# Attention ahead of a mixture of experts on one core: part of the softmax subtraction and of the key sums goes to ScalarE, two buffers for token lists, a new order of issue

## The chip, the cores and the metric

The kernel runs on one core of one Trainium2 chip. The metric is device time in microseconds (us), the median of several runs. The engines are TensorE (PE, with its weight loads shown apart as PEld), VectorE (DVE), ScalarE (ACT), GpSimd (POOL) and SyncE (SP), whose queue issues most transfers. Each engine works through its own instructions in the order in which they were issued, and waits on semaphores for the others.

## What is computed

```python
# q, k, v: 8 x 8 heads x 576 x 64; keys and values are averaged over groups of 8 rows
k_p = k.reshape(B, H, Sp, pool, D).mean(axis=3)
v_p = v.reshape(B, H, Sp, pool, D).mean(axis=3)
scores = scale * np.matmul(q, k_p.transpose(0, 1, 3, 2))
scores = scores - np.max(scores, axis=-1, keepdims=True)
attn = np.exp(scores)
attn = attn / (np.sum(attn, axis=-1, keepdims=True) + 1e-09)
x = np.matmul(attn, v_p)                       # then heads side by side: 8 x 576 x 512
...
logits = x @ w_gate; local_gate = sigmoid(x @ w_local)
# along each sequence: token s takes argmax(logits[s]), or the expert before it if local_gate >= 0.5
h = np.maximum(x[b, s] @ w1[e], 0.0)           # 512 -> 1024
out[b, s] = p[e] * (h @ w2[e])                 # 1024 -> 512, p = softmax(logits)
```

## The kernel before

The work has two halves. **Attention** runs in 20 units (four pairs of batches, five units each: `t` from 0 to 3 is one batch with 128 query rows twice, `t == 4` stacks the remaining rows of both batches). A unit is a chain: `sc` puts its scores into one PSUM tile `sp` of three banks, of which there is one; `mx` takes the row maxima on DVE (864 columns of banks 0 and 1, 288 of bank 2); `sb` subtracts them on DVE from PSUM into `ap`; `ex` takes the exponential on ACT from `ap` into `at`; `T0`, `T1`, `T2` transpose `at` on PE and `T0c`... copy the results to SBUF; `v0`, `v1`, `v2` multiply by the values on PE and `v0c`... copy those; `fs`, `fp`, `fd` scale and store the rows. The same value product gives the routing logits. Beside the units run the keys (`lk` loads, `kp` sums over groups of 8 on DVE into `kd`, and into the half empty tile `kdz`), the values (`lv` loads, `vp` sums on POOL or, as `vp.d`, on DVE, `vt`, `vc`, `vl`, `vd` turn them through the gate weights, `vm` on POOL or `vm.d` on DVE places them into `vaug`), the routing of each pair (`rA`, `rT0` to `rP`), 36 scatters of token numbers (`s`, POOL) and the first expert's weights (`w1`, `w2` load; `p1`, `p2` split each number into a high part, copied on ACT, and a low part, subtracted on POOL, or on DVE as `p1.d`, `p2.d`).

**Experts** follow: blocks of 256 tokens of one expert, `L1` and `L2` for the first, then `M1`, `M2`, then a chain of blocks in `blocks(b)`. Each block's token numbers come by `ids_load` from SP into `idp`, `meta` adds them up on DVE, `gather` fetches the rows, `quarters` and `x_turn` turn them.

What sets the order is a list written out by hand, `PLAN` for attention, `PLAN_B` and `PLAN_C` for the passage to the experts: `do(name, n)` issues step `name` of unit, chunk or pair `n`, in the list's order. A suffix (`.d`, `.p`, `.s`) sets `pick["e"]`, the engine that takes the step. So each engine's queue is the list's steps of that engine, in that order. For instance, around the third pair's routing the list says

```python
v1:14 T1c:15 T2:15 w1:3 vl:21 v1c:14 sc:17 vd:21 T2c:15 ex:16 fs:14 vl:23 ga:0 fp:14 vd:23 p1:2 v0:15 rA:2 T0:16
v0c:15 p1:3 v1:15 T0c:16 T1:16 v1c:15 mx:17 XR:0 v2:15 rT0:2 fd:14 v2c:15 sb:17 T1c:16 rT1:2 vp:22 rS0:2 fs:15
```

Of the kernel before, what the change touches and what calls it, by code (L numbers as in the profile page):

```python
# [16 lines left out]
P = 128  # L17
# [38 lines left out]
wa:0 lv:0 lv:1 lv:2 lk:0 wa:1 lk:1 lk:2 lq:0 lc:0 lq:1 lq:2 lq:3 vp:0 vp.d:2 lv:3 vt:0 vc:0 vm:0 vt:2 kp:0  # L56
vc:2 vm:2 vp:1 lk:3 kp:1 lv:4 vt:1 lv:5 kp:2 vm:1 lk:4 sc:0 lk:5 vl:0 mx:0 lq:4 vc:1 vd:0 sb:0 vl:2 vd:2 ex:0 vl:1
sc:2 vd:1 T0:0 mx:2 T0c:0 T1:0 vp:3 sb:2 v0:0 T1c:0 T2:0 kp:3 v1:0 v0c:0 T2c:0 lv:6 vt:3 v1c:0 v2:0 vm.d:3 vp:5
vc:3 lk:6 vl:3 v2c:0 sc:1 vp:4 ex:2 vd:3 fs:0 vt:5 lq:5 lq:6 T0:2 mx:1 vc:5 fp:0 lv:7 lv:8 vt:4 vl:5 vm.d:5 vc:4
vm:4 T0c:2 vd:5 kp:4 vl:4 fd.p:0 T1:2 vd:4 vp:6 v0:2 kp:5 lk:7 T1c:2 T2:2 v0c:2 v1:2 T2c:2 kp:6 lv:9 lk:8 v1c:2  # L60
v2:2 sb:1 lk:9 vt:6 v2c:2 vm:6 fs:2 ex:1 sc:3 fp:2 vc:6 mx:3 lq:7 T0:1 vp:8 T1:1 T0c:1 sb:3 fd.p:2 v0:1 T1c:1 vp:7
T2:1 kp:7 v1:1 v0c:1 T2c:1 ex:3 v2:1 vp:9 lv:10 lv:11 lk:10 v1c:1 sc:4 v2c:1 T0:3 lq:8 fs:1 vl:6 lv:12 T0c:3 T1:3
vd:6 vt:8 fp:1 mx:4 T1c:3 vm.d:8 vc:8 sb:4 T2:3 fd.p:1 vt:7 T2c:3 kp:8 vl:8 vc:7 sc:5 vm:7 ex:4 vd:8 kp:9 lk:11
v0:3 lq:10 T0:4 v0c:3 mx:5 vp:11 lk:12 v1:3 T0c:4 vp:10 T1:4 sb:5 v1c:3 v2:3 T1c:4 vl:7 v2c:3 vt:9 vd:7 ex:5 vt:11
fs:3 sc:6 lv:14 lv:13 vm:11 vc:11 vm.d:9 vc:9 fp:3 vl:11 lq:9 pf:0 mx:6 T0:5 vt:10 fd.p:3 T0c:5 vd:11 v0:4 kp:10 vc:10
# [38 lines left out]
def moe_attention(ctx: ExitStack, tc: tile.TileContext, q, q_st, k, v, w_gates, w1, w2, out):  # L104
# [23 lines left out]
    scratch_i = const.tile([P, 64], I32, name="scratch_i")  # L128
# [3 lines left out]
    nc.gpsimd.iota(scratch_i[:, 0:2 * E], pattern=[[0, 2], [1, E]], base=0, channel_multiplier=0)  # L132
    nc.vector.tensor_copy(out=iota8, in_=scratch_i[:, 0:2 * E].rearrange("p (b e) -> p b e", b=2))
# [107 lines left out]
    idp = route.tile([P, 4, TB, 2], F32, name="idp", bufs=1)  # L241
# [956 lines left out]
```

## Time and profile before

| what | value |
|---|---|
| median of 3 runs | 669.05 us (664.52 to 671.4) |
| profiled execution, its own time | 667.99 us |
| its span, first to last instruction | 665.9 us |
| PE busy | 614.6 us, 92% of the span |
| DVE busy | 444.5 us, 67% |
| ACT busy | 272.5 us, 41% |
| POOL busy | 249.8 us, 38% |
[...]

The page's picture in 40 slices of 16.6 us shows where the halves differ: PE's digits run between 4 and 9 in the first 13 slices and stand at 9 from there to the end; the granted clock shows 6, 7 and 8 in places of the first 13 slices and full speed after. The chain that ended last is, in the end, the last scatter of output rows (L1063). Idle time of an engine counts only where the bottleneck waits for it, so the views that matter are PE's waits, by stretch.

### The profile page before, as it was taken

To read this page: it belongs to the slowest core of one execution; us is meant where nothing else is said; L and a number is where in the kernel's file an instruction comes from. 1 tells how busy PE (TensorE), PEld (TensorE's weight loads), DVE (VectorE), ACT (ScalarE), POOL (GpSimd) and SP (SyncE) were. 2 spreads that over 40 slices of the span, in tenths; PEclk is the share of its full clock that TensorE was granted. 3 is DMA by queue.
4 is the path that set the end of the run, shared out by engine and by line. 5 is a ranking of instruction groups with operands and counts; after the bars stand their busy time and mean duration, and the time that the engine had idled before them with its cause. 6 is when DMAs were issued, how large, how long until landed. Compare 5 with 4: busy or idle time off the path is not lost. (4 is left out here: it accounts for less than half of the span.)

```text
span 665.9 us, 11834 instructions
## 1 busy us (share of the span) xinstructions
PE 614.6 (92%) x3588; PEld 520.8 (78%) x3588; DVE 444.5 (67%) x1002; ACT 272.5 (41%) x612; POOL 249.8 (38%) x297
## 2 busy tenths in 40 slices
PE   4889898987787999999999999999999999999994
PEld 3777797876575888878888878788887887888883
DVE  7688989887677744454549448578944478954550
ACT  1354454444463242132336226366713266522330
POOL 6477767767475532121112221211222112222102
PEclk9998999976698999999999999999999999999998
DMA  8799946364413036953237644948864329764222
GB/s 326 270 354 343 319 171 206 127 207 128 143 40 104 11 83 173 329 162 114 69 108 240 224 125 109 331 117 320 280 211 126 110 65 335 251 230 121 78 93 61
DMA packets 74966, 120.12 MB, mean 180 GB/s; under 512 B 21486, under 2 KB 42994, under 8 KB 74868
## 3 DMA queue, kind: packets, MB, share of 16 engines
q1 hardware_dynamic: 66196, 96.41, 43.3%
q0 software_dynamic: 8672, 22.59, 10.8%
q8 instruction: 39, 0.64, 0.4%
q14 instruction: 59, 0.48, 0.2%
HBM read 87.85 MB, written 33.22 MB: 182 GB/s over the span
## 5 line engine op out<-in xcount | busy, mean ns | idle before, releaser
L327 PE MATMUL hp<-x,w1h 128*128 128x512 f32 x376 | 135.8, 402 | 0.1
L348 PE MATMUL o_ps<-w2h,ht_h 128*128 128x512 f32 x312 | 122.7, 393 | 1.5 <-PEq L1128 0.9
L348 PE MATMUL o_ps<-w2h,ht_l 128*128 128x512 f32 x312 | 122.0, 391 | 0.0
L348 PE MATMUL o_ps<-w2l,ht_h 128*128 128x512 f32 x312 | 121.6, 390 | 0.0
L306 POOL DMA_INDIRECT kk<-x_rows,mi x44 | 43.9, 997 | 186.7 <-DVE mi L302 172.1
L329 PE MATMUL hp<-x,w1l 128*128 128x256 f32 x376 | 106.2, 282 | 0.4 <-DVE w1l L212 0.4
L334 ACT COPY hs<-hp 128x256 f32<-128x256 f32 x94 | 34.8, 371 | 145.0 <-PE hp L329 143.1
L327 PEld LDWEIGHTS hp<-x,w1h 128*128 128x128 f32 x376 | 71.3, 190 | 17.8 <-DVE hs L335 0.6
L564 PE MATMUL op<-vaug,aT 128*128 128x148 f32 (+4 forms) x448 | 73.9, 326 | 2.1 <-ACT aT L373 1.8
L329 PEld LDWEIGHTS hp<-x,w1l 128*128 128x128 f32 x376 | 71.7, 191 | 1.4 <-DVE w1l L212 0.8
L564 PEld LDWEIGHTS op<-vaug,aT 128*128 128x128 f32 (+1 forms) x448 | 66.0, 193 | 7.9 <-ACT aT L373 3.1
L339 ACT ACTIVATE ht_h<-hs 128x256 fp32r<-128x256 f32 x136 | 57.2, 420 | 34.7 <-DVE hs L335 34.6
L348 PEld LDWEIGHTS o_ps<-w2h,ht_h 128*128 128x128 f32 x312 | 58.6, 188 | 14.6 <-ACT ht_h L960 2.5
L348 PEld LDWEIGHTS o_ps<-w2h,ht_l 128*128 128x128 f32 x312 | 58.6, 188 | 13.4 <-DVE ht_l L961 0.7
L348 PEld LDWEIGHTS o_ps<-w2l,ht_h 128*128 128x128 f32 x312 | 58.6, 188 | 11.5
L340 DVE SCALAR_TENSOR_TENSOR ht_l<-hs,ht_h 128x256 fp32r<-128x256 f32 x136 | 59.2, 435 | 6.3 <-ACT ht_h L339 6.0
L335 DVE TENSOR_TENSOR hs<-hp,hs 128x256 f32<-128x256 f32 x94 | 38.9, 418 | 28.4 <-ACT hs L334 27.6
L1063 POOL DMA_INDIRECT out<-ob,mi x22 | 24.9, 1130 | 72.7 <-DVE ob L1060 33.0
L1060 DVE TENSOR_SCALAR ob<-o_ps,ms 128x512 f32<-128x512 f32 x22 | 16.5, 749 | 52.5 <-PE o_ps L348 51.7
L1063 POOL DMA_INDIRECT out<-vt_in,mi x20 | 23.8, 1192 | 65.7 <-DVE vt_in L1060 19.4
L373 ACT COPY osb<-op 128x444 f32<-128x444 f32 (+2 forms) x56 | 26.5, 476 | 48.1 <-PE op L564 43.6
L700 POOL DMA_INDIRECT ids<-pm,pos x36 | 35.9, 998 | 23.9 <-DVE pos L697 12.7
(245 smaller groups left out, 1129.1 us busy)
## 6 DMA issues: line engine op xcount, KB each, us to landing
raw<-in_moe_w SPq DMA_DIRECT2D x56, 512.0 KB
xd<-kk SPq DMA_DIRECT2D x21, 512.0 KB
kt<-xd SPq DMA_DIRECT2D x84, 128.0 KB
kk<-in_k SPq DMA_DIRECT2D x16, 576.0 KB
vt_in<-in_v SPq DMA_DIRECT2D x16, 512.0 KB
qt<-in_q SPq DMA_DIRECT2D x16, 512.0 KB
x_rows<-xs SPq DMA_DIRECT2D x16, 512.0 KB
vt_in<-in_v SPq DMA_DIRECT2D x16, 128.0 KB
```

The costliest lines, as they stand in the source:

```text
L306: nc.gpsimd.indirect_dma_start(out=xg[b % 2][:, h, :], out_offset=None, in_=x_rows[0:NT + 1], in_offset=bass.IndirectOffsetOnAxis(ap=mi[b ...
L327: nc.tensor.matmul(out=ps, lhsT=W1[0][:, kk, f * P:(f + 1) * P], rhs=xt[:, kk].rearrange("p i n -> p (i n)"), start=(kk == 0), stop=False, ...
L329: nc.tensor.matmul(out=ps[:, 0:2 * P], lhsT=W1[1][:, kk, f * P:(f + 1) * P], rhs=xt[:, kk, 0, :], start=False, stop=(kk == KD - 1), skip_g ...
L334: nc.scalar.copy(out=hb[:, 0, :], in_=ps[:, 2 * P:])
L335: nc.vector.tensor_tensor(out=hb[:, 1, :], in0=ps[:, 0:2 * P], in1=hb[:, 0, :], op=ALU.add)
L339: nc.scalar.activation(out=ht[0][:, f, :], in_=hb, func=AF.Relu)
L340: nc.vector.scalar_tensor_tensor(out=ht[1][:, f, :], in0=hb, scalar=0.0, in1=ht[0][:, f, :].bitcast(F32), op0=ALU.max, op1=ALU.subtract)
L348: nc.tensor.matmul(out=to[h], lhsT=ht[i][:, kk, h * P:(h + 1) * P], rhs=W2[j][:, kk, :], start=(n == 0), stop=(n == 3 * KF - 1))
L373: nc.scalar.copy(out=out, in_=in_)
L564: nc.tensor.matmul(out=out, lhsT=lhs, rhs=rhs if len(out.shape) == 3 else rhs.rearrange("p s x -> p (s x)"), start=all(x[0] != n for x in ...
L700: nc.gpsimd.indirect_dma_start(out=ids[u % 4].rearrange("t m w -> (t m) w"), out_offset=bass.IndirectOffsetOnAxis(ap=pos[:, u:u + 1], axis=0),
L1063: nc.gpsimd.indirect_dma_start(out=outv, out_offset=bass.IndirectOffsetOnAxis(ap=mi[b % NM][:, h:h + 1], axis=0), in_=ob[b % 2][:, h, :], ...
```

## The change

Four things are done. First, a unit's `sb` step may be marked `sb.a`: then DVE subtracts only bank 2 (288 columns), ACT makes a tile `nm` of twelve negated, scaled maxima, and ACT's exponential reads banks 0 and 1 straight from PSUM in twelve instructions of 72 columns, each with its own column of `nm` as bias; ten of the 16 wide units are marked (0, 2, 3, 6, 7, 10, 11, 12, 13, 16). Second, DVE sums all of a key chunk in one instruction of 144 groups, and the two halves of `kdz` are copied from `kd` by ACT. Third, `idp` gets two buffers, taken in turn. Fourth, `PLAN` and `PLAN_B` are written in a new order, with other engines for some steps: `vm.d` stands 4 times instead of 10, `p2.d` 4 times and `p1.d` once instead of never, and 15 PSUM copies (`vc.d`, `T2c.d`, `v0c.d`, `v1c.d`, `v2c.d`) are marked for DVE. `PLAN_C` is the same.

```diff
 PLAN = plan("""
-wa:0 lv:0 lv:1 lv:2 lk:0 wa:1 lk:1 lk:2 lq:0 lc:0 lq:1 lq:2 lq:3 vp:0 vp.d:2 lv:3 vt:0 vc:0 vm:0 vt:2 kp:0
...
+lv:0 lk:1 lk:0 lv:5 vp:0 kp:1 kp:0 vp:5 vm:5 lq:0 sc:0 lk:6 kp:6 lv:2 vp.d:2 vt:2 vc:2 vt:0 wa:0 wa:1 vc:0 mx:0 sb.a:0
...
+L1:1 L1:0 L1:2 h0:1 L1:4 XR:1 rA:3 h0:0 h1:1 rT0:3 rS0:3 rT1:3 h1:0 L1:3 h0:2 h1:2 h0:4 rS1:3 rT2:3 L2:0 rE:3 L2:8
...
-    idp = route.tile([P, 4, TB, 2], F32, name="idp", bufs=1)
+    idps = [route.tile([P, 4, TB, 2], F32, name=f"idp{i}", bufs=1) for i in range(2)]
...
-            m = 2 - cc
-            nc.vector.tensor_reduce(out=kd[bb % NBUF][:, 2 * cc:2 * cc + m, :].rearrange("p h g -> p (h g)"),
-                                    in_=kv[:, 0:m * G], axis=AX.X, op=ALU.add)
+            nc.vector.tensor_reduce(out=kd[bb % NBUF][:, 2 * cc:2 * cc + 2, :].rearrange("p h g -> p (h g)"), in_=kv, axis=AX.X, op=ALU.add)
             if cc:
                 for hh in range(2):
-                    nc.vector.tensor_reduce(out=kdz[bb % NBUF][HALF[hh], hh, :], in_=kv[HALF[hh], G:2 * G], axis=AX.X, op=ALU.add)
+                    nc.scalar.copy(out=kdz[bb % NBUF][HALF[hh], hh, :], in_=kd[bb % NBUF][HALF[hh], 3, :])
...
-            for sv, mv, av, shp in views:
+            wide = pick["e"] != "a"
+            if not wide:
+                nm = ap2.tile([P, 12], F32, name="nm")
+                nc.scalar.activation(out=nm, in_=mx[:, 0:12], func=AF.Copy, scale=-1.0 / (POOL * 8.0))
+            for sv, mv, av, shp in views if wide else views[1:]:
                 nc.vector.tensor_tensor(out=av, in0=sv, in1=mv.unsqueeze(3).broadcast_to(shp), op=ALU.subtract)
...
+                else:
+                    for n in range(12):
+                        kb, j, i = n // 6, n // 3 % 2, n % 3
+                        nc.scalar.activation(out=main[:, j, kb * c + i * G:kb * c + (i + 1) * G], in_=sp[:, kb, n % 6 * G:(n % 6 + 1) * G],
+                                             func=AF.Exp, bias=nm[:, n:n + 1], scale=1.0 / (POOL * 8.0))
...
-        ids_load(bass.ds(entry(b + 4, 1, (EN.SP,), NU32 - TB), TB))
+        ids_load(bass.ds(entry(b + 4, 1, (EN.SP,), NU32 - TB), TB), b + 4)
```

The order on three engines shows what moved. On DVE at unit 16 of attention, before (`mx` and `ap` are its maxima and its subtraction, `xs` the scaling of rows, `vaug` the placing of values):

```order
L442 TENSOR_TENSOR vaug_215<-vs,mk 128x2x64
L442 TENSOR_TENSOR vaug_215<-vs,mk 128x3x64
L488 TENSOR_REDUCE mx<-sp 128x12
L488 TENSOR_REDUCE mx<-sp 128x4
L601 TENSOR_TENSOR xs<-osb,rr 128x512
L491 TENSOR_TENSOR ap<-sp,mx 128x864
L491 TENSOR_TENSOR ap<-sp,mx 128x288
```

and DVE at the same unit with the change (`w2l` is the low part of a weight chunk, `rr`, `lgx`, `lg` belong to `fs`):

```order
L216 TENSOR_TENSOR w2l<-vt_in,w2h 128x1024
L431 TENSOR_TENSOR vaug_215<-rt,mk 128x3x9 x2
L608 TENSOR_TENSOR xs<-osb,rr 128x512 x2
L485 TENSOR_REDUCE mx<-sp 128x12
L485 TENSOR_REDUCE mx<-sp 128x4
L431 TENSOR_TENSOR vaug_216<-rt,mk 128x2x9
L431 TENSOR_TENSOR vaug_216<-rt,mk 128x3x9
L588 TENSOR_SCALAR rr<-osb 128x16
L589 RECIPROCAL rr<-rr 128x16
L591 TENSOR_TENSOR lgx<-osb,rr 128x144
L594 TENSOR_REDUCE lg<-lgx 128x2x9
L374 COPY vT<-tp 128x128
```

The wide subtraction and the placing of values have left DVE here; a weight chunk and copies out of PSUM have come.

On ACT at the exponential of unit 16, before (`aT` and `osb` are copies that PE's next steps wait for, `w1h` a weight chunk):

```order
L373 COPY aT<-tp 128x512
L373 COPY osb<-op 128x148
L373 COPY aT<-tp 128x128
L506 ACTIVATE at<-ap 128x2x2x216
L506 ACTIVATE at<-ap 128x2x80
L506 ACTIVATE at<-ap 128x128
L211 CAST w1h<-kt 128x1024
```

and ACT there with the change:

```order
L490 ACTIVATE nm<-mx 128x12
L372 COPY osb<-op 128x444
L372 COPY osb<-op 128x148
L506 ACTIVATE at<-sp,nm 128x72 x12
L513 ACTIVATE at<-ap 128x2x80
L513 ACTIVATE at<-ap 128x128
L372 COPY osb<-op 128x444 x2
L372 COPY aT<-tp 128x512
```

One instruction of 864 columns has become twelve of 72, and two copies stand between `nm` and the first of them.

On POOL where the first expert's weights are split, before:

```order
L212 TENSOR_TENSOR w1l<-kt,w1h 128x1024
L217 TENSOR_TENSOR w2l<-vt_in,w2h 128x1024
L260 MEMSET qt 128x1024
L264 DMA qt<-x_rows,idr_196 128x512 x2
L601 TENSOR_TENSOR xs<-osb,rr 128x256
L212 TENSOR_TENSOR w1l<-kt,w1h 128x1024 x2
```

and POOL there with the change:

```order
L707 DMA ids_64<-pm,pos 65536x2
L211 TENSOR_TENSOR w1l<-kt,w1h 128x1024
L439 TENSOR_TENSOR vaug_216<-vs,mk 128x2x64
L211 TENSOR_TENSOR w1l<-kt,w1h 128x1024
L608 TENSOR_TENSOR xs<-osb,rr 128x512 x2
L259 MEMSET qt 128x1024
```

Of the eight weight subtractions of attention, three stay on POOL and five are DVE's now.

## Rows read from the trace of the kernel before

**Rows 1.** Windows: length, busy of PE, PEld, DVE, ACT, POOL; clock, DMA.

```profile
0.00:200.45 200.45, 165.59 (x1360) 145.51 (x1361) 163.41 (x382) 90.45 (x217) 135.12 (x189) 0.91 0.64 220
200.45:222.78 22.33, 18.29 (x96) 15.01 (x94) 16.43 (x56) 6.91 (x21) 11.87 (x13) 0.85 0.21 65
222.78:665.90 443.12, 430.75 (x2138) 360.30 (x2136) 264.66 (x565) 175.15 (x375) 102.77 (x97) 1.00 0.52 168
```

**Rows 2.** Waits of PE, 0 to 223 us: total, times, longest.

```profile
PE sp L459 <- DVE ap L491: 12.2, 7, 4.2
PE tp L420 <- POOL vs L381: 5.4, 2, 2.8
PE rt L426 <- DVE vaug L434: 5.2, 5, 1.5
...
PE op L564 <- DVE vaug L434: 0.3, 1, 0.3
```

**Rows 3.** The longest wait of PE from 222.8 us on.

```profile
PE hp L958 <- ACT hs L955: 1.1, 2, 0.5
```

**Rows 4.** The longest wait of SP's queue, whole span.

```profile
SPq L294 <- DVE mi L302: 89.0, 12, 11.8
```

**Rows 5.** Groups by line and form, 0 to 250 us: count, busy, mean ns, idle before.

```profile
L491 DVE TENSOR_TENSOR ap<-sp,mx 128x864 f32<-128x864 f32 x16 | 16.7, 1044 | 0.0
L506 ACT ACTIVATE at<-ap 128x864 f32<-128x864 f32 x16 | 14.9, 929 | 7.3 <-DVE ap L491 7.3
L403 DVE TENSOR_REDUCE kdz<-kk 64x72 f32<-64x576 f32 x16 | 11.9, 741 | 0.1
L399 DVE TENSOR_REDUCE kd<-kk 128x144 f32<-128x1152 f32 x8 | 10.7, 1341 | 0.1
L399 DVE TENSOR_REDUCE kd<-kk 128x72 f32<-128x576 f32 x8 | 5.9, 738 | 0.0
L373 ACT COPY osb<-op 128x444 f32<-128x444 f32 x36 | 19.1, 529 | 41.8 <-PE op L564 37.3 <-issue 3.7 <-POOL vs L381 0.7
L442 DVE TENSOR_TENSOR vaug<-vs,mk 128x192 f32<-128x192 f32 x8 | 5.6, 721 | 0.0
L442 DVE TENSOR_TENSOR vaug<-vs,mk 128x128 f32<-128x128 f32 x8 | 5.0, 631 | 0.0
L373 ACT COPY vT<-tp 128x128 f32<-128x128 f32 x16 | 4.2, 266 | 13.7 <-PE rt L426 7.6 <-PE tp L420 6.1
L652 ACT ACTIVATE pe<-sh 128x72 f32<-128x72 f32 x4 | 1.0, 262 | 0.0
```

**Rows 6.** The same view, 222 to 640 us: weight subtraction on DVE.

```profile
L217 DVE TENSOR_TENSOR w2l<-raw,w2h 128x1024 fp32r<-128x1024 f32 x24 | 28.4, 1220 | 0.5
```

**Rows 7.** Timeline of DVE: start, length, instruction, and idle before it.

```profile
160.94 2.67 DVE L620 TENSOR_TENSOR sh<-lg,ml 128x72 f32<-128x72 f32 x1
163.65 0.23 DVE L621 SCALAR_TENSOR_TENSOR eq<-sh,iota8m 128x72 f32<-128x72 f32 x1
...
168.46 1.41 DVE L488 TENSOR_REDUCE mx<-sp 128x12 f32<-128x864 f32 x2
...
170.13 1.41 DVE L491 TENSOR_TENSOR ap<-sp,mx 128x864 f32<-128x864 f32 x2
```

**Rows 8.** Timeline of POOL at the same place.

```profile
161.16 2.36 POOL L212 TENSOR_TENSOR w1l<-kt,w1h 128x1024 fp32r<-128x1024 f32 x1
```

**Rows 9.** Timeline of PE: start, length, instruction, idle before it.

```profile
96.06 1.45 PE L564 MATMUL op<-vaug,aT 128*128 128x148 f32 x8
97.34 0.60 PE L522 MATMUL tp<-ident,at 128*128 128x128 f32 x4
...
156.04 1.33 PE L459 MATMUL sp<-kdz,qt 128*128 128x144 f32 x4 [4.15 <-DVE ap L491]
...
171.59 1.33 PE L459 MATMUL sp<-kdz,qt 128*128 128x144 f32 x4 [3.23 <-DVE ap L491]
...
211.79 0.50 PE L643 MATMUL tp<-ident,ab 128*2 128x128 f32 x2 [2.64 <-DVE erow L648]
```

More of the change, by code (lines that the diff above doesn't have):

```diff
@@ L61 @@
[L61 to L65, printed above, removed]
@@ new lines @@
+v2:5 vl:10 lv:17 lq:10 kp:8 T0:6 vd:10 T0c:6 sc:7 kp:10 rE:0 v2c:5 T1:6 T1c:6 vt:12 vc:12 fs:5 lv:15 mx:7 rL:0 rO:0
+lq:12 T2:6 T2c:6 vp:13 sb.a:7 ex:7 fp:5 fd.p:5 vt:14 vc:14 kp:9 v0:6 v1:6 v1c:6 lv:21 v0c:6 vm:16 pf:0 rR:0 rV:0 rP:0
+lk:15 sc:8 mx:8 vp:17 vm.d:17 sb:8 lq:11 T2:7 T2c:7 vl:12 T0:7 T0c:7 v2:6 vd:12 vp:15 T1:7 T1c:7 fp:4 fd.p:4 v2c:6
+v0:7 v2:7 v0c.d:7 sc:9 vl:14 lq:14 ex:8 T1:8 T1c:8 vd:14 T0:8 lv:20 vm:14 mx:9 sb:9 T2:8 v1:7 lv:23 T2c.d:8 vm:15
+lk:14 fs:6 fp.d:6 T0c:8 ex:9 T0:9 vt:13 vc:13 T0c:9 sc:10 v1c:7 fd:6 T1:9 v2c:7 T1c:9 v0:9 v1:9 kp:15 v0c:9 mx:10
@@ new lines @@
+w2:3 vm:18 w1:2 v1:11 T1:12 v1c:11 rR:1 rV:1 rP:1 T0:12 T0c:12 sc:13 T1c:12 T2:12 T2c:12 v2:11 mx:13 v2c:11 vt:18
+lq:16 fs:10 v0:12 vc:18 vl:18 s:0 s:0 vt:20 sb.a:13 ex:13 w2:0 v1:12 s:0 s:0 fp:10 fd.p:10 s:0 s:0 s:0 vd:18 vc:20
+v1c:12 kp:12 sc:14 mx:14 fs:11 vl:20 vd:20 T1:13 T0:13 v0c:12 T1c:13 sb:14 T0c:13 v2:12 v2c:12 fs:12 v0:13 fp:12 vt:19
+vc:19 fd.p:12 T2:13 T2c:13 lq:18 vp.d:22 ex:14 sc:15 T1:14 vm:22 T1c:14 v1:13 mx:15 sb:15 v0c:13 p2.d:3 T0:14 vt:21
+w2:1 vl:19 vd:19 T0c:14 s:0 s:0 s:0 v2:13 v2c:13 fp.d:11 fd:11 vc:21 sc:16 mx:16 w1:3 ex:15 T1:15 T0:15 vl:21 vd:21
@@ L126, in moe_attention @@
                             compare_op=ALU.is_equal, fill=0.0, base=0, channel_multiplier=-1)
-    scratch_i = const.tile([P, 64], I32, name="scratch_i")
+    scratch_i = const.tile([P, 16], I32, name="scratch_i")
     iota8 = const.tile([P, 2, E], F32, name="iota8")
@@ L131, in moe_attention @@
     ebase = const.tile([P, 2, E], F32, name="ebase")
-    nc.gpsimd.iota(scratch_i[:, 0:2 * E], pattern=[[0, 2], [1, E]], base=0, channel_multiplier=0)
-    nc.vector.tensor_copy(out=iota8, in_=scratch_i[:, 0:2 * E].rearrange("p (b e) -> p b e", b=2))
+    nc.gpsimd.iota(scratch_i, pattern=[[0, 2], [1, E]], base=0, channel_multiplier=0)
+    nc.vector.tensor_copy(out=iota8, in_=scratch_i.rearrange("p (b e) -> p b e", b=2))
     nc.vector.tensor_scalar(out=iota8m, in0=iota8, scalar1=float(-E), scalar2=None, op0=ALU.add)
@@ L290, in rows_split, with ids_load @@
         nc.vector.tensor_tensor(out=xt[:, cs, 1, :], in0=tv, in1=xt[:, cs, 0, :].bitcast(F32), op=ALU.subtract)
-    def ids_load(r):
+    def ids_load(r, b):
         for u in range(4):
-            nc.sync.dma_start(idp[:, u].rearrange("p j w -> p (j w)"),
+            nc.sync.dma_start(idps[b % 2][:, u].rearrange("p j w -> p (j w)"),
                               ids[u][:, r, :].rearrange("t j w -> t (j w)").unsqueeze(0).broadcast_to([4, 32, 2 * TB]))
     def meta(b):
-        nc.vector.tensor_reduce(out=ids4, in_=idp.rearrange("p u j w -> p j w u"), axis=AX.X, op=ALU.add)
+        nc.vector.tensor_reduce(out=ids4, in_=idps[b % 2].rearrange("p u j w -> p j w u"), axis=AX.X, op=ALU.add)
         nc.vector.tensor_tensor(out=picked.rearrange("p h w j -> p h j w"),
@@ L360, in moe_attention @@
         vaug = [ap1.tile([P, VOFF[-1], SEG], F32, name=f"vaug{i}") for i in range(NBUF)]
-        kd = [ap1.tile([P, 3, G], F32, name=f"kd{i}") for i in range(NBUF)]
+        kd = [ap1.tile([P, 4, G], F32, name=f"kd{i}") for i in range(NBUF)]
         kdz = [ap1.tile([P, 2, G], F32, name=f"kdz{i}") for i in range(NBUF)]
@@ L472, in scores @@
                             kb = (2 * pr + b) % NBUF
-                            rhs = kd[kb][HALF[hh], i, :] if i < 3 else kdz[kb][HALF[hh], hh, :]
-                            nc.tensor.matmul(out=sp[r, hh, i * G:(i + 1) * G], lhsT=qT[HALF[hh], 0, i, r], rhs=rhs, start=True, stop=True)
+                            nc.tensor.matmul(out=sp[r, hh, i * G:(i + 1) * G], lhsT=qT[HALF[hh], 0, i, r], rhs=kd[kb][HALF[hh], i, :],
+                                             start=True, stop=True)
             yield
@@ L496, in scores @@
                 last = ap[:, 4 * c:].rearrange("p (j x) -> p j x", j=2)
-                moves = ((main[:, :, 0:2 * c].rearrange("p j (k x) -> p k j x", k=2),
-                          ap[:, 0:4 * c].rearrange("p (k j x) -> p k j x", k=2, j=2)),
-                         (main[:, :, 2 * c:MAIN], last[:, :, 0:MAIN - 2 * c]),
+                moves = ((main[:, :, 2 * c:MAIN], last[:, :, 0:MAIN - 2 * c]),
                          (at[:, 2 * MAIN:].rearrange("p (j c) -> p j c", j=2), last[:, :, MAIN - 2 * c:]))
+                if wide:
+                    moves = ((main[:, :, 0:2 * c].rearrange("p j (k x) -> p k j x", k=2),
+                              ap[:, 0:4 * c].rearrange("p (k j x) -> p k j x", k=2, j=2)),) + moves
+                else:
[3 more added lines that the diff above has]
+                                             func=AF.Exp, bias=nm[:, n:n + 1], scale=1.0 / (POOL * 8.0))
             else:
```

67 lines of the change are left out of this document (30 added, 37 removed).

## The prediction, made blind

> **What bounds the kernel now.** First the windows [rows 1]. From 222.78 us on PE is busy 430.75 of 443.12 us at full granted clock, and its longest wait with a name there is 1.1 us in total [rows 3]: the experts are bound by PE's work, which the change doesn't touch, since it adds and removes no matmul. Up to 222.78 us PE is busy 165.59 + 18.29 = 183.9 us, so it idles 38.9 us, and its granted clock is 0.91 and 0.85 of full speed, which costs some 0.09 x 165.6 + 0.15 x 18.3 = 17.6 us more. Everything that can be won or lost lies in these 56 us. The reader's next view is therefore PE's waits in that stretch [rows 2]. Twelve us wait for `sp`, the one score tile, until DVE's subtraction `ap` releases it; with the seven smaller groups that DVE ends (placing values, routing scans, sums; the smallest 0.3 us), DVE is the late one in some 27 us of the 38.9. POOL ends 5.4 us. DVE itself is busy 163.41 of the first 200.45 us, against 90.45 of ACT and 135.12 of POOL. So attention is a ring of PE and DVE in which DVE is most often late, and the timeline shows the two largest single waits, 4.15 and 3.23 us, around the third pair's routing [rows 9].
>
> **What leaves DVE and what comes.** By [rows 5]: ten subtractions of 864 columns leave, 10 x 1.044 = 10.4 us. The sixteen half sums for `kdz` leave, 16 x 0.741 = 11.9, and eight key sums grow from 72 to 144 groups, 8 x (1.341 - 0.738) = 4.8 back. Ten placings of values go to POOL, six of 192 and four of 128 columns: 6 x 0.721 + 4 x 0.631 = 6.9. To DVE come fifteen copies out of PSUM, which ACT makes in 0.27 to 0.53 us each; DVE shows no such copy, and at ACT's price they are some 5 us (from nothing gained to twice that: 4 to 10). Five weight subtractions come at 1.22 [rows 6], 6.1 us, and smaller moves of about 1 us. Balance: 10.4 + 11.9 - 4.8 + 6.9 - 5 - 6.1 - 1 = 12 us less for DVE before the experts.
>
> **What DVE loses beside POOL.** The subtraction `sh` of 72 columns at 160.94 took 2.67 us, where the next instruction, of the same size, took 0.23 [rows 7]; it ended as POOL's weight subtraction of 2.36 us from 161.16 ended [rows 8]. So an instruction on DVE can stand until POOL is done. Of eight such stretches on POOL five go. One may cost DVE nothing or 2.4 us, so five are worth 0 to 12; I take 1 us each, 5 us, nearer the low end since the instruction that comes then must be of the kind that waits. With this DVE is relieved of 17 us.
>
> The five weight subtractions that come to DVE could stand in the same way, each behind a POOL instruction of 2.36 us [rows 8]: 5 x 2.36 = 12 us of the 17 would be gone. This is a rival below. [...]
>
> **How much of the 17 us reaches the path.** Nothing, if PE is then late itself; all of it, if DVE is always late. DVE ends 27 of PE's 38.9 idle us, but not the rest, and in busy stretches a DVE that is early helps nobody, so I take half, 8.5 us, and keep 0 and 17 for the range. The low clock follows the waits (0.91 over the first stretch, 1.00 where PE doesn't wait, [rows 1]); with fewer waits I give back 3 of its 15 us there, between 0 and 10.
>
> **The chain through ACT.** A marked unit pays in latency. Before, after the maxima (1.41 us for both) come the subtractions (1.41) [rows 7] and one exponential of 0.929 [rows 5]. Now come `nm` and twelve exponentials of 72 columns. The nearest row is ACT's exponential of 72 columns, 0.262 us [rows 5]: 0.26 + 12 x 0.262 = 3.4 us, so `at` is ready 3.4 - 1.41 - 0.93 = 1.1 us later, and `sp` is released 4.8 us after the scores are done (1.41 + 3.4) in place of 2.8. One of the twelve could cost as little as its share of columns, 0.929 / 12 = 0.08, or as much as the copy of 444 columns from PSUM, 0.529: 1.2 to 6.6 us in all; I take 0.262, the same function and size. Nobody sees this where PE has enough other rows between two score groups. I counted the matmuls there in the new order, at 1.28 us for a value group and half a microsecond for four transposes [rows 9]: after units 6, 7, 11, 12 and 16 they make 5.6 to 8.3 us, after 2 and 10 some 4.9, after 3 and 13 only 3.9. So two units fall short by 1 us each: 2 us lost. ACT's queue holds the copies that PE needs, `aT` and `osb`, behind the twelve; ACT gains about 25 us of work (10 x 2.5, the `kdz` copies 16 x 0.25, less the copies that leave) on 90.45 in 200 us, so it isn't the bound, but the copies come later. That is in the first rival.
>
> **The start and the end of attention.** At the start two value loads no longer stand ahead of the keys and queries, which helps the first scores; but the first unit is a marked one with only 1.2 us of PE work before the next scores want `sp`. I take 0, between 3 gained and 3 lost. At the end the fourth pair's routing runs beside the first expert: PE waits 4.0 us there, 2.64 of it for one scan [rows 9], and its clock is 0.85, another 2.7 us [rows 1]. The new order puts second-layer matmuls between the routing steps, which can cover waits: 3 of these 6.7 us, between 0 and 6.
>
> **The token lists.** With one buffer, SP stands 89.0 us in total at the load that `meta` must free [rows 4]; two buffers take this away. But hardly anybody on PE waits behind it: all of PE's idle time after 222.78 us is 443.12 - 430.75 = 12.4 us, the end of the program after its last matmul included, and no group of its waits there is over 1.1 us [rows 3]. I put it at 0, and at most 4.
>
> **Sum.** 8.5 + 3 + 3 - 2 = 12.5 us off the profiled execution's own 667.99 us gives 655.5. The median of the runs shown is 1 us higher, so 656 us, 1.9% faster than 669.05.
>
> **Rivals.** *The twelve exponentials become the bound (slower).* If ACT's queue is late in the marked units, PE waits for `sp` 2.0 us longer in each, and for `aT` 1.1 longer: 10 x 3.1 = 31 us lost against the 14.5 won above, 685 us; if only `sp` matters and the clock gives nothing back, 20 lost against 11.5, 677. It decides from the point where PE's cover after the scores is under 4.8 us, or the copies ahead of the twelve on ACT add the difference. Against it: the counted cover, and ACT's load. For it: the two copies that stand between `nm` and the exponentials of unit 16, and the units with 3.9 us. *PE and POOL keep the time (no change).* POOL takes the ten placings and all but a few of the row scalings; if its sums of values, which PE waited for in [rows 2], or the loads set the pace, the relief of DVE isn't seen, and only the end counts: 669 - 3 = 666. *The weight subtractions stand behind POOL.* Then 17 - 12 = 5 us of relief are left, half of it 2.5, and the sum is 2.5 + 3 + 3 - 2 = 6.5: 662 against the median. For it speaks the row of 2.67 us; against it, that POOL keeps only three of its own long subtractions. *The order packs well (much faster).* With all 17 us, half the clock loss, 7.5, and 5 at the end, 29 us less: 639 on the execution's own time; as a case, 639 to 649.
>
> **How the numbers follow.** This kernel's runs differ by up to 1%, so a difference under 1% (662.4 to 675.7 us) can't be told from none. Forecast, 649 to 662: 0.50. Much faster: 0.14. Weight subtractions behind POOL, 660 to 665, half of it inside 1%: 0.08. No change: 0.17. Slower by the ACT chain, 675 to 685: 0.11. That gives faster 0.50 + 0.14 + 0.04 = 0.68, same 0.17 + 0.04 = 0.21, slower 0.11. The range that holds 8 in 10 leaves out half of the much faster case and the slow one: 644 to 670.
>
> **What would show it.** In the changed profile: twelve exponentials of about 0.26 us each on ACT; DVE's busy time before the first expert matmul near 147 us in place of 163; that first matmul between 185 and 193 us in place of 200.45; the two waits of 4.15 and 3.23 us smaller; the stretch after PE becomes dense still 443 us long. The prediction is wrong if PE's waits for `sp` grow, now ended by ACT, or if the waits on DVE only give way to waits on POOL.

## The result, and the profile after

The changed kernel takes 640.47 us (median of four runs, 637.69 to 645.85) against 666.78 us of the kernel before on the same chip: a ratio of 0.9615, with an interval of 0.951 to 0.9719. In a later series it was 642.58 us, 0.9602 (0.9561 to 0.9643). The forecast was 656 us. Some executions of a kernel run in a slower state; the ratios leave these out, the medians hold all. The profiled execution took 645.85 us, the longest of the four, with a span of 643.8; before, 667.99 and 665.9.

The windows of the changed kernel, cut at the first expert matmul and, as in [rows 1], 22.33 us behind it (length, busy of PE, PEld, DVE, ACT, POOL; clock, DMA share, GB/s):

```profile
0.00:179.47 179.47, 154.62 (x1361) 138.17 (x1361) 146.95 (x358) 106.46 (x336) 125.00 (x189) 0.96 0.74 247
179.47:201.80 22.33, 18.18 (x97) 14.46 (x95) 19.29 (x56) 7.69 (x20) 14.05 (x14) 0.92 0.19 60
201.80:643.80 442.00, 429.97 (x2136) 359.70 (x2134) 266.36 (x575) 175.32 (x377) 102.72 (x99) 0.99 0.53 169
```

The first expert matmul starts at 179.47 instead of 200.45 us. In the 22.33 us behind it PE makes 97 matmuls, before 96, and the rest takes 442.0 us, before 443.12. So 21.0 us are gained ahead of the experts. Two parts make them up: PE's idle time up to the dense stretch falls from 38.9 to 24.85 + 4.15 = 29.0 us, and its busy time, for the same matmuls, from 183.9 to 172.8, at a granted clock of 0.96 and 0.92 in place of 0.91 and 0.85 (busy time times clock is 166.2 us before and 165.2 after).

In a second trace of the same kernel, of 638.57 us from the later series, the first expert matmul starts at 170.49 us:

```profile
0.00:170.49 170.49, 147.13 (x1361) 130.54 (x1361) 145.01 (x358) 106.15 (x336) 125.04 (x189) 0.99 0.78 260
```

So the gain ahead of the experts lies between 21 and 30 us; the medians differ by 26.3.

PE's waits in the changed kernel, 0 to 201 us (total, times, longest):

```profile
PE sp L456 <- ACT kdz L400: 10.6, 1, 10.6
PE sp L470 <- ACT at L506: 2.3, 2, 1.9
PE tp L529 <- ACT at L513: 2.2, 4, 0.6
PE rt L423 <- DVE vaug L431: 2.2, 3, 1.4
...
PE sp L456 <- ACT at L506: 1.2, 2, 0.6
```

The first row is the start of the kernel, one wait until the first scores can run; before, they began at 13.24 us. Behind it stands no group over 2.3 us where [rows 2] has 12.2, 5.4 and 5.2. The units at which PE stood 4.15 and 3.23 us [rows 9] have their scores with no wait now, and unit 18 comes 11.5 us earlier (PE's timeline):

```profile
153.14 0.66 PE L456 MATMUL sp<-kdz,qt 128*128 128x144 f32 x4
...
160.07 0.70 PE L456 MATMUL sp<-kdz,qt 128*128 128x144 f32 x4
```

The new instructions, by line and form, 0 to 230 us (count, busy, mean ns, idle ahead):

```profile
L506 ACT ACTIVATE at<-sp,nm 128x72 f32<-128x72 f32 x120 | 26.5, 354 | 7.2 <-DVE ap L492 5.0 <-DVE rr L588 2.1 <-DVE vaug L431 0.2
L397 DVE TENSOR_REDUCE kd<-kk 128x144 f32<-128x1152 f32 x16 | 21.4, 1343 | 0.7 <-DMA kk<-in_k 0.7
L211 POOL TENSOR_TENSOR w1l<-kt,w1h 128x1024 fp32r<-128x1024 f32 x3 | 7.7, 2576 | 2.6 <-ACT w1h L210 2.5
L216 DVE TENSOR_TENSOR w2l<-vt_in,w2h 128x1024 fp32r<-128x1024 f32 x4 | 6.3, 1566 | 0.0
```

One exponential of 72 columns lasts 354 ns, but the next begins before it ends: 26.5 us for ten dozen are 2.65 us a dozen, 0.22 each.

### The profile page after: what moved, and what is told of

The parts are those of the page before. It is cut to its first block, busy times and chain, and to the rows that moved or that the text cites. A ratio compares the mean times of both kernels' runs of the same rounds, so it can differ in the third digit from the quotient of the medians.

```text
span 643.8 us, 11923 instructions
## 1 busy us (share of the span) xinstructions
PE 602.8 (94%) x3588; PEld 512.3 (80%) x3588; DVE 432.6 (67%) x987; ACT 289.5 (45%) x733; POOL 241.8 (38%) x301
## 5 line engine op out<-in xcount | busy, mean ns | idle before, releaser
L571 PE MATMUL op<-vaug,aT 128*128 128x148 f32 (+6 forms) x448 | 67.4, 314 | 0.0
L571 PEld LDWEIGHTS op<-vaug,aT 128*128 128x128 f32 (+2 forms) x448 | 62.2, 185 | 3.4 <-issue 1.2
L1067 DVE TENSOR_SCALAR ob<-o_ps,ms 128x512 f32<-128x512 f32 x22 | 16.5, 748 | 50.6 <-PE o_ps L347 50.6
L1070 POOL DMA_INDIRECT out<-vt_in,mi x20 | 22.5, 1123 | 66.0 <-DVE vt_in L1067 19.4
L707 POOL DMA_INDIRECT ids<-pm,pos x36 | 37.8, 1050 | 15.7 <-issue 8.3
L319 ACT CAST x<-qt 128x512 fp32r<-128x512 f32 x40 | 24.0, 611 | 42.9 <-DVE qt L314 42.9
```

What stands on the lines that cost most here:

```text
L319: nc.scalar.copy(out=xt[:, cs, 0, :], in_=xr_t[:, cs, :])
L571: nc.tensor.matmul(out=out, lhsT=lhs, rhs=rhs if len(out.shape) == 3 else rhs.rearrange("p s x -> p (s x)"), start=all(x[0] != n for x in ...
L707: nc.gpsimd.indirect_dma_start(out=ids[u % 4].rearrange("t m w -> (t m) w"), out_offset=bass.IndirectOffsetOnAxis(ap=pos[:, u:u + 1], axis=0),
L1070: nc.gpsimd.indirect_dma_start(out=outv, out_offset=bass.IndirectOffsetOnAxis(ap=mi[b % NM][:, h:h + 1], axis=0), in_=ob[b % 2][:, h, :], ...
```

## The experiments

"Steps" below are the two things computed otherwise (ten subtractions by ACT, key sums in one piece); "engines" are the marks that choose an engine in the list of attention, "sequence" is its order without them. Beside the marks named above, the list also moves, for instance, row scalings: `fp` of six units to DVE, `fd` of six to POOL. "The new order" is the new list with its engines. Each ratio is to the kernel before, timed in the same series.

**The new steps in the old order.** The new key sums, and ten units of the old list are marked; four exponentials move, since a marked unit's must be read from `sp` ahead of the next scores. Unit 15 is marked in place of unit 12, which can't be there. The text below counts five exponentials; units 2, 6, 11 and 16 are meant.

```diff
-... v0c:4 sb:6 ... v1c:4 T2:5 sc:7 T2c:5 ex:6 ...
+... v0c:4 sb.a:6 ... v1c:4 T2:5 ex:6 sc:7 T2c:5 ...
```

> The old order of issue with the new steps: ten units take the exponential from PSUM on ACT (0, 2, 3, 6, 7, 10, 11, 13, 15, 16; five of their exponentials stand just ahead of the next scores, since the score tile must be read first), the key sums in one instruction, two token buffers; weight subtractions, value placings and copies stay on their old engines. If the relief of VectorE makes the gain whatever the order is: 640 to 652 us. If the order makes it: 658 to 668 us. If the longer chain through ACT costs in an order that wasn't written for it: over 668.

Measured: 702.8 us, 1.0511 (1.0463 to 1.0559). Its window up to the first expert matmul, PE's longest waits for `sp` in it, and one place of PE's timeline:

```profile
0.00:231.63 231.63, 181.63 (x1361) 159.34 (x1361) 148.17 (x356) 112.24 (x353) 135.53 (x189) 0.85 0.56 191
```

```profile
PE sp L460 <- ACT at L510: 21.4, 8, 4.9
...
PE sp L460 <- DVE ap L496: 4.3, 2, 3.1
PE sp L474 <- ACT at L510: 3.9, 2, 2.1
```

```profile
82.38 1.33 PE L460 MATMUL sp<-kdz,qt 128*128 128x144 f32 x4 [4.93 <-ACT at L510]
```

DVE has 148.17 us of work in place of 163.41, a relief of 15 us, and the kernel is 5% slower: PE stands 25.3 us for `sp` until ACT's exponentials are done. This is the slower rival of the prediction, in an order that gives PE too little between a marked unit and the next scores.

**The new order with the old steps.** All `sb.a` become `sb`, and the key sums are the old ones.

```diff
-... wa:1 vc:0 mx:0 sb.a:0
+... wa:1 vc:0 mx:0 sb:0
...
-    nc.scalar.copy(out=kdz[bb % NBUF][HALF[hh], hh, :], in_=kd[bb % NBUF][HALF[hh], 3, :])
+    nc.vector.tensor_reduce(out=kdz[bb % NBUF][HALF[hh], hh, :], in_=kv[HALF[hh], G:2 * G], axis=AX.X, op=ALU.add)
```

> The new order with the old steps: all 16 wide units are subtracted on VectorE and the keys are summed in three instructions, which puts 17 us of work back on VectorE (10 x 1.04 + 16 x 0.74 - 8 x 0.60); two token buffers, weight subtractions and copies as in the changed kernel. If the order makes the gain: 640 to 650 us. If the relief makes it: 655 to 668 us.

Measured: 642.62 us, 0.9606 (0.9561 to 0.9651), the time of the changed kernel. Its window up to the first expert matmul:

```profile
0.00:173.61 173.61, 149.68 (x1360) 133.75 (x1360) 158.57 (x384) 85.13 (x200) 124.71 (x189) 0.99 0.77 255
```

DVE carries 158.57 us here, 91% of the stretch, and ends 10.4 us of PE's waits in it, where it ended 23.6 before. So the gain needs none of the relief from the steps; the new list, order and engines together, brings it.

**The old passage to the experts.** `PLAN_B` of before, all else changed.

```diff
-L1:1 L1:0 L1:2 h0:1 L1:4 XR:1 rA:3 ...
+rA:3 L1:0 h0:0 h1:0 L1:1 h0:1 L1:2 rT0:3 ...
```

> The changed kernel with the old order of the passage to the experts, the new one in attention. If the passage gives the 3 us that were predicted for it: 643 to 646 us, against 640.5 for the changed kernel. If attention alone makes the gain: within 1.5 us of the changed kernel. If the passage makes more than half: over 653.

Measured: 643.71 us, 0.9631 (0.9579 to 0.9684). The new passage can't be told from nothing; the 3 us given to it can be neither seen nor excluded.

**The weights' subtractions back on POOL**, all five, in the changed kernel, and later in the version without twelve exponentials.

```diff
-... mx:15 sb:15 v0c:13 p2.d:3 ... fp:16 fd.p:16 T1:18 ga:1 p1.d:1 ...
+... mx:15 sb:15 v0c:13 p2:3 ... fp:16 fd.p:16 T1:18 ga:1 p1:1 ...
```

> The changed kernel with the five weight subtractions back on GpSimd. If instructions on VectorE stood behind GpSimd's long subtractions before and that was a good part of the gain: 645 to 652 us, with single VectorE instructions of 2 us and more beside them. If it was not: within 2 us of the changed kernel's 640.5, or faster, since VectorE has 6 us less to do.

> The changed kernel with all wide subtractions on VectorE and the five weight subtractions on GpSimd. If GpSimd's queue is what the sequence is tuned around, as the stall of 7.4 us behind GpSimd in the run with the new sequence alone suggests: 643 to 655 us. If the cost of 5 us in the changed kernel came with the twelve exponentials: 637 to 641.

Measured: 647.85 us, 0.968 (0.9633 to 0.9728), and 643.0 us, 0.9659 (0.9598 to 0.972), against 0.9615 and 0.9557 with them on DVE: some 4 to 7 us. The intervals of the first pair overlap, those of the second don't. They are better on DVE.

**Two token buffers alone**, in the kernel before.

```diff
-    idp = route.tile([P, 4, TB, 2], F32, name="idp", bufs=1)
+    idps = [route.tile([P, 4, TB, 2], F32, name=f"idp{i}", bufs=1) for i in range(2)]
```

> The kernel before with two buffers for the token lists and nothing else. If SP's 89 us of waiting for the list's reader delay nothing that PE waits for: within 1% of the kernel before, 665 to 671 us. If they delay weights or rows: 655 to 663 us.

Measured: 667.97 us, 0.9968 (0.9925 to 1.0011): nothing, as forecast, though SP's wait of 89.0 us [rows 4] was the longest of its queue.

**The sequence and the engines apart.** First the new sequence with every step on its old engine, then the old sequence with the new engines, both with the old steps.

```diff
-... lc:0 vm.d:0 vm:2 ... T2c.d:0 v2:0 ...
+... lc:0 vm:0 vm:2 ... T2c:0 v2:0 ...
```

> Only the sequence of the list is new: old steps (all wide subtractions and three key sums on VectorE), and every step on the engine that it had before (ten value placings on VectorE, weight subtractions on GpSimd, copies on ScalarE); two token buffers. If the sequence alone makes the gain: 638 to 646 us. If the choice of engines makes half of it, with the weights (5 us, measured) as a part: 648 to 656. If the engines make it all: 660 to 670.

> The old sequence and the old steps, with each step on the engine that the new list gives it: value placings on GpSimd, five weight subtractions and fifteen PSUM copies on VectorE, row scalings as in the new list; two token buffers. If the engines make the gain: 640 to 652 us. If the sequence makes it: 660 to 672. If they only work together: about the time before, 667 to 670.

Measured: 658.58 us, 0.9871 (0.9814 to 0.9927), and 670.47 us, 1.0043 (1.0009 to 1.0078). With the old steps the four cases are then 1 (old sequence, old engines), 1.0043 (old, new), 0.9871 (new, old) and 0.9606 (new, new): the new engines cost a little in the old sequence and give 2.65% in the new one. PE's timeline of the new sequence on old engines shows the longest wait behind the start, and POOL's what stands ahead of it:

```profile
113.84 3.85 PE L577 MATMUL op<-vaug,aT 128*128 128x222 f32 x12 [7.39 <-POOL vaug L445]
```

```profile
110.17 1.47 POOL L713 DMA_INDIRECT ids<-pm,pos  x1 [1.12 <-DMA ids<-pm,pos]
...
113.28 1.02 POOL L445 TENSOR_TENSOR vaug<-vs,mk 128x192 f32<-128x192 f32 x2
```

A placing on POOL stands behind scatters of token lists, and PE waits 7.4 us for it. The old placings alone, among the other new engines, cost nothing (below), so it takes more than their engine.

The traces also show where each part works. These are the windows from the scores of unit 16 to the first expert matmul: the kernel before, the old sequence with new engines, the new sequence with old engines, the new order with the old steps, and the changed kernel.

```profile
146.09:200.45 54.36, 43.23 (x336) 37.21 (x335) 41.11 (x88) 28.39 (x62) 35.26 (x27) 0.81 0.32 101
155.95:204.53 48.58, 39.82 (x336) 33.69 (x335) 39.16 (x83) 26.22 (x54) 21.64 (x23) 0.86 0.31 104
151.50:189.35 37.85, 35.85 (x335) 32.05 (x335) 34.29 (x75) 26.41 (x58) 30.04 (x25) 0.95 0.50 155
136.58:173.61 37.03, 34.48 (x335) 30.81 (x334) 35.71 (x81) 27.04 (x58) 26.62 (x23) 1.00 0.59 184
142.37:179.47 37.10, 34.66 (x336) 30.75 (x335) 34.93 (x80) 28.54 (x70) 26.82 (x23) 1.00 0.58 179
```

The new sequence shortens this stretch by 16.5 us on the old engines and by 11.5 on the new; in all runs of this document that were traced it lasts 36.5 to 39.7 us with the new second half of the list and 48.6 to 56.5 with the old. The new engines work ahead of it: in the new sequence they bring unit 16's scores from 151.50 to 136.58 us.

**One group of engines or steps at a time, in the new order.** All sixteen subtractions on DVE (`sb.a` to `sb`, new key sums kept), and this again beside the changed kernel itself; the placings of values on their old engines; with the wide subtraction, the fifteen copies back on ACT; and with the wide subtraction, the old placings.

```diff
-... wa:1 vc:0 mx:0 sb.a:0
+... wa:1 vc:0 mx:0 sb:0
...
-lv:0 lk:1 lk:0 lv:5 vp:0 kp:1 kp:0 vp:5 vm:5 ...
+lv:0 lk:1 lk:0 lv:5 vp:0 kp:1 kp:0 vp:5 vm.d:5 ...
...
-... v0:0 T2c.d:0 v2:0 ...
+... v0:0 T2c:0 v2:0 ...
```

> The changed kernel with all 16 wide subtractions on VectorE; the key sums stay in one instruction with ScalarE's copies. If VectorE's time still ends PE's waits in the new order: 643 to 650 us. If PE's own work and order bound it: 637 to 642 us, with the copies that stood behind the twelve exponentials earlier.

> The changed kernel with the value placings on the engines that they had before (ten on VectorE, others on GpSimd), 7 to 10 us of VectorE work more and as much less on GpSimd. If the new sequence counts on GpSimd for them: 648 to 655 us. If the weights alone (5 us, measured) and the copies were what the sequence counts on: within 2 us of the changed kernel.

> The changed kernel once more, beside the next one, on the same chip: 638 to 645 us.

> The changed kernel with all wide subtractions on VectorE, once more, beside the changed kernel on the same chip. If the twelve exponentials cost time in the new order too: 3 us or more below the changed kernel. If not: within 2 us of it.

> The changed kernel with all wide subtractions on VectorE and all fifteen PSUM copies on ScalarE. If the sequence counts on VectorE for copies: 644 to 652 us, where with the copies on VectorE it was 638. If ScalarE has the room: 636 to 641.

> The changed kernel with all wide subtractions on VectorE and the value placings on the engines that they had before, each of which alone gave about 638 us. If both gains add: 634 to 637 us. If VectorE is then late: 640 us or more.

Measured: wide subtraction 637.79 us, 0.9558 (0.9506 to 0.9611), again 638.41, 0.9557 (0.9531 to 0.9584), beside 642.58, 0.9602 (0.9561 to 0.9643) of the changed kernel in one series; old placings 638.86, 0.9568 (0.9545 to 0.9591); copies on ACT 639.23, 0.9596 (0.9541 to 0.9652); wide subtraction and old placings 637.59, 0.956 (0.9508 to 0.9612). Undone alone in the new order, none of these edits costs anything that can be measured. The twelve exponentials give nothing or lose 4 us (the intervals touch). Wide subtraction with the old key sums is the new order with the old steps, 0.9606 (0.9561 to 0.9651): the new key sums give nothing or 3 us, and the two steps together come to nothing.

**Routing moved behind the maxima**, in the kernel before: `mx` and `sb` of units 7, 12 and 17 ahead of the routing of pairs 0, 1 and 2.

```diff
-... fp:4 rA:0 vl:10 ... v0:5 mx:7 rT0:0 v0c:5 sb:7 ...
+... fp:4 mx:7 sb:7 rA:0 vl:10 ... v0:5 rT0:0 v0c:5 ...
```

> The kernel before, where the maxima and the subtraction of units 7, 12 and 17, whose scores are already out, stand ahead of the first routing step of their pair on VectorE (some 5 us of small instructions each) instead of behind it. If these three places are a good part of the old order's loss, since the score tile then comes free 5 us earlier: 655 to 662 us, with the wait of 3.2 us at unit 18 gone. If the loss is spread over the whole list, or PE then waits for the routing instead: 664 to 670.

Measured: 672.5 us, 1.004 (1.0008 to 1.0071). PE's waits, 0 to 205 us:

```profile
PE sp L462 <- DVE ap L494: 9.9, 6, 4.1
PE rt L429 <- DVE vaug L437: 8.5, 6, 3.4
...
PE tp L646 <- DVE ab L631: 3.5, 1, 3.5
```

Against [rows 2] the wait for the subtraction falls by 2.3 us, that for the placings grows by 3.3, and 3.5 us for the routing stand beside them. The wait of 3.23 us at unit 18 is gone, and the stretch from unit 16's scores to the first expert matmul is 50.25 us in place of 54.36, but these scores come at 153.82 us in place of 146.09. What DVE does later is then late.

**Half of the order.** With wide subtraction, new key sums and new engines: the new list up to the scores of unit 11 and the old one from there (with the old passage), and the other way round. At the seam stand, in the order of the second list, the steps that it has ahead of its place and the first hadn't had. Of the first, against the new list:

```diff
-... lk:13 fs:7 v0:8 v0c.d:8 v1:8 sc:11 vd:13 v1c:8 s:0 ...
+... lk:13 fs:7 v0:8 v0c.d:8 v1:8 lk:12 lv:18 s:0 ... v1c:8 v2:8 vm:13 vd:13 vt:15 sc:11 ...
```

> The new list up to the scores of unit 11, then the old list's order for all that is left, and the old passage; all steps on the new list's engines, all wide subtractions on VectorE, keys in one instruction. If the second half of attention holds the gain, since the first half reaches unit 11 at about the same time in both (100.4 and 97.4 us): 658 to 668 us. If the first half's extra work done ahead holds it: 640 to 648.

> The old list's order up to the scores of unit 11, then the new order for all that is left, and the new passage; engines and steps as in the run before this. If the second half holds the gain: 638 to 648 us. If the new second half counts on work that only the new first half has done: 655 to 668.

Measured: 671.55 us, 1.0093 (1.0055 to 1.0132), and 648.95 us, 0.9767 (0.9687 to 0.9847), with 0.9557 for the whole new order. So the second half alone brings some half of the gain, and the first half alone nothing, but neither is a clean test: at the first one's seam PE stands 6.82 us once until DVE's `rr`, and the seam of the other may cost part of what is missing. From unit 16's scores to the first expert matmul the first takes 48.68 us and the second 37.04, as long as the whole new order.

**The waits filled.** In the kernel before PE repeats matmuls whose result is the same, ahead of the scores of units 17 and 18.

```diff
-            nc.tensor.matmul(out=mp[:, 0:m * H * GL], ...
+            for _ in range(14 if (bb, cc) == (7, 0) else 1):
+                nc.tensor.matmul(out=mp[:, 0:m * H * GL], ...
...
-                for i in range(2):
+                for i in list(range(2)) * (5 if (pr, half) == (2, 1) else 1):
```

> The kernel before with PE's two longest waits, 4.15 us ahead of unit 17's scores and 3.23 us ahead of unit 18's, filled with repeats of the matmuls that stand just ahead of them (14 of the gate product, 5 of the second routing transposes), which write the same numbers again. If PE's low clock from 150 to 180 us (0.55 to 0.94 there) comes from these two idle stretches and costs time: granted clock near 1 there, and 660 to 665 us. If the low clock costs nothing since PE waits anyway: 667 to 671 us.

Measured: 665.53 us, 0.9985 (0.9947 to 1.0024), between the two cases. The window 150 to 180 us, of the kernel before, then of this one with its two fillings in PE's timeline, then of the changed kernel:

```profile
150.00:180.00 30.00, 21.27 (x129) 17.78 (x125) 21.84 (x42) 12.87 (x28) 16.80 (x13) 0.68 0.48 149
```

```profile
150.00:180.00 30.00, 24.69 (x205) 20.30 (x204) 23.73 (x48) 15.13 (x31) 20.32 (x15) 0.94 0.48 151
```

```profile
152.54 3.60 PE L427 MATMUL rt<-wg,vT 128*128 128x144 f32 x28
...
165.54 4.01 PE L644 MATMUL tp<-ident,ab 128*2 128x128 f32 x20 [1.66 <-ACT aT L373]
```

```profile
150.00:180.00 30.00, 27.56 (x263) 24.77 (x263) 27.86 (x66) 23.64 (x60) 20.71 (x18) 1.00 0.51 161
```

With work in the two longest waits the granted clock of these 30 us is 0.94 in place of 0.68, in one trace of each, and the time is the same within 0.5%, 3.5 us. If PE were late throughout these 30 us, the clock of 0.68 would cost 0.32 x 21.27 = 6.8 us (an estimate from the first line), and this is ruled out. A smaller gain is not: in the trace with the fillings, unit 16's scores to the first expert matmul take 50.06 us in place of 54.36.

Elsewhere a low clock does show in the time. In the new order with wide subtraction one wait of 2.15 us ends at 144.29 us, and in the lap from the scores of unit 17 to those of unit 18 that follows PE works without a break:

```profile
144.79:154.92 10.13, 10.13 (x68) 9.40 (x66) 9.34 (x27) 6.59 (x12) 7.16 (x5) 0.66 0.40 107
```

The new order with the old steps needs 7.57 us at 1.00 for the same matmuls (shown below). So a lap in which PE is late took 2.6 us more at a clock of 0.66. The lap behind it is 1.6 us shorter in return, 6.82 against 8.38, since a wait of PE for DVE, 1.52 us in the new order with the old steps, falls away there. The changed kernel has a full clock from 150 to 180 us and a PE that is busy 27.56 of those 30 us, all with work that has to be done.

## Why the prediction was wrong

**What was right.** The sign; the place (ahead of the experts, whose dense stretch is 442 us long); the token buffers at nothing; and that the five weight subtractions wouldn't all stand behind POOL. Four of them take 1.21 to 1.23 us, as in [rows 6], and one 2.62, where the rival gave each 2.36 more. The last two on DVE's timeline:

```profile
180.20 1.22 DVE L216 TENSOR_TENSOR w2l<-vt_in,w2h 128x1024 fp32r<-128x1024 f32 x1
184.45 2.62 DVE L216 TENSOR_TENSOR w2l<-vt_in,w2h 128x1024 fp32r<-128x1024 f32 x1
```

DVE's busy time before the first expert matmul, 147 us forecast and 146.95 measured, was met in part by luck: all five weight subtractions were counted in, and these two come behind that matmul. Of the 5 us, an estimate, for instructions that stand behind POOL no balance can be seen: `sh` falls from 3.8 to 1.5 us, but `po` rises from 0.8 to 3.1 and `rr` from 4.1 to 6.8. The first expert matmul itself came at 179.47 us, ahead of the 185 to 193 that were named as a sign.

**The step that failed is "How much of the 17 us reaches the path".** It priced the change as relief of DVE, halved it to 8.5 us, gave 3 us of clock back, and left the order only 3 us at the end of attention. The runs turn this round. With 15 us of relief in the old order the time grows by 5%; with the old steps back on DVE in the new order it is the same as with the change. The traces point to when each engine gets its work between one unit's scores and the next. These are the windows from the scores of unit 16 to those of 17, 17 to 18, and 18 to 19, first of the kernel before, then of the new order with the old steps:

```profile
146.09:156.04 9.95, 5.80 (x66) 4.48 (x64) 9.85 (x15) 5.93 (x14) 8.63 (x6) 0.89 0.26 75
156.04:171.59 15.55, 11.51 (x68) 10.23 (x69) 11.89 (x26) 6.82 (x14) 9.78 (x8) 0.72 0.29 92
171.59:190.88 19.29, 17.63 (x130) 15.54 (x133) 13.12 (x32) 9.44 (x20) 9.80 (x6) 0.75 0.39 123
```

```profile
136.58:146.33 9.75, 9.29 (x88) 7.99 (x87) 9.54 (x22) 6.42 (x14) 6.72 (x6) 1.00 0.90 287
146.33:153.90 7.57, 7.19 (x68) 6.58 (x66) 7.29 (x21) 6.49 (x12) 6.76 (x5) 1.00 0.61 179
153.90:162.70 8.80, 7.28 (x91) 6.66 (x94) 8.45 (x20) 5.10 (x13) 5.40 (x6) 1.00 0.39 107
```

Before, DVE is busy 9.85 of 9.95 us in the first lap while PE has 5.80; two laps later PE has 17.63 of 19.29 and DVE 13.12. One engine is full while the other waits, and then the other way round. In the lap between, both have nearly the same work, 11.51 and 11.89 of 15.55 us, and still wait for each other, since the third pair's routing stands ahead of unit 17's maxima on DVE [rows 7]; so equal sums in a lap aren't enough either. In the new order PE and DVE have nearly the same work in each lap, and PE is busy at least 83% of it and DVE 96%. A sum of DVE's work over the whole stretch, from which the prediction argued, doesn't show this: over the stretch DVE was busy 163.41 of 200.45 us, 82%, and in the new order with the old steps it is 158.57 of 173.61, 91%.

**The terms.** The clock was given 3 us back; PE's busy time fell by 11.1, over half of the 21.0 gained in this trace, so this term was far too small. How much of it the clock alone would bring isn't known; filling two of the waits brought 3.5 us at most. The order's end was given 3 us; the old passage costs 1 to 2, within the noise, and PE still idles 4.15 us there, before 4.04. The chain through ACT was given 2 us lost, behind units 3 and 13; PE waits 3.5 us for `sp` on ACT, behind units 3, 7, 10 and 13. In time it is 0 to 4 us in the new order, where a dozen takes 2.65 us instead of the 3.14 assumed; in the old one such waits are over 25 us. The relief given as 8.5 us is 0 for the steps (0.9606 without them). Of the engines' 2.65%, some 17 us, the weight subtractions make 4 to 7; the copies and the placings, each alone, nothing; the row scalings weren't tried alone.

**The rivals.** "The order packs well" gave 639 to 649 us, and that is the time, but its working, all 17 us of DVE's relief, isn't what happened. "The twelve exponentials become the bound" is a real mechanism, with 21.4 us of such waits in the old order; the new order gives PE enough to do behind a marked unit. "PE and POOL keep the time" was wrong: POOL's sums of values held PE 5.4 us [rows 2], and no group ended by POOL is among the longest in the changed kernel; with the new sequence on the old engines POOL did hold PE, 7.4 us once.

On the weights, single instructions on DVE do last longer beside a subtraction on POOL, and others don't. In the new order with the old steps one `w2l` on DVE takes 3.30 us beside a `w1l` of 2.35 on POOL, while four of the five on DVE in the changed kernel take 1.21 to 1.23 (timelines of DVE and of POOL):

```profile
152.42 3.30 DVE L216 TENSOR_TENSOR w2l<-vt_in,w2h 128x1024 fp32r<-128x1024 f32 x1
152.29 2.35 POOL L211 TENSOR_TENSOR w1l<-kt,w1h 128x1024 fp32r<-128x1024 f32 x1
```

In the kernel before, the two maxima at 151.82 us take 1.41 us together beside a `w2l` of 2.34 on POOL, and 1.42 at 140.29 with no subtraction there:

```profile
140.29 1.42 DVE L488 TENSOR_REDUCE mx<-sp 128x12 f32<-128x864 f32 x2 [0.93 <-PE sp L465]
...
151.82 1.41 DVE L488 TENSOR_REDUCE mx<-sp 128x12 f32<-128x864 f32 x2
```

```profile
151.76 2.34 POOL L217 TENSOR_TENSOR w2l<-vt_in,w2h 128x1024 fp32r<-128x1024 f32 x1
```

But the weights still cost less on DVE than on POOL, where one takes 2.576 us; whether such lengthening or only POOL's queue makes the 4 to 7 us, no run here tells.

**Still open:** which steps of the second half carry the gain. Neither the routing's place alone nor the two longest waits alone do, and whether the new second half needs the new first half for its last 2% (0.9767 against 0.9557), or the seam took them, wasn't told apart. At least some 10 us of the engines' share belong to no group of marks that was tried alone. The key sums without the exponentials weren't tried in the old order, so its loss of 5% is that of both steps together. The balance of the laps is read from traces and wasn't changed by itself; the halves and the four cases of sequence and engines show only that the list makes the gain, and where.

**A faster version:** the new order, engines and key sums, with all subtractions wide on DVE, 0.9557 (0.9531 to 0.9584) against 0.9602 (0.9561 to 0.9643) of the change; the intervals touch.

## What to carry to other kernels

Where engines work in a ring over one buffer, cut the trace into laps of that ring, compare the engines' work lap by lap, and read the waits inside a lap; a sum over the stretch shows an engine as the bound that is only badly mixed with the others. Price a new order apart from the work that moves with it, and try each without the other: here the order with its engines is worth 4%, the steps nothing, and the steps in the old order cost 5%. Don't price a low clock around waits apart from these waits: filling two of them in the old order won 3.5 us at most, where the clock alone was estimated at 6.8. But look at the laps behind a wait too: one of them took 2.6 us more at a clock of 0.66, without any wait of its own, and 1.6 came back in the next.

## What the runs showed of the hardware

In the changed kernel small exponentials from PSUM overlap on ACT: each of 72 columns lasts 354 ns, but ten dozen make ACT busy for 26.5 us, 221 ns each. TensorE's granted clock over 30 us was 0.94 of full speed in a trace with some 6.5 us of repeated matmuls in PE's waits (of the 3.60 and 4.01 us above, 13 of 14 and 4 of 5 parts) and 0.68 in one without them, with no change of the time beyond 0.5%. And after a single wait of 2.15 us a lap of matmuls ran at a mean of 0.66 and took 10.13 us, where the new order with the old steps took 7.57 at 1.00. Beside a subtraction of 2.35 us on POOL one of the same size on DVE took 3.30 us, where four of the changed kernel's five took 1.21 to 1.23.
